# W1 in thirds, the first two tiles in column pieces, and the final waits on GpSimd: one change to a linear-attention and MLP kernel

## Chip, cores, metric

One core of one Trainium2 chip. The metric is the device time of one execution in microseconds (us), and lower is better.

## The reference, cut to what matters

```python
x = A_x                                  # 1 x 2048 x 640, bf16
xn = _layernorm(x, axis=-1)
return x + _A_ref(xn, A_wqkv, A_wo) + _B_ref(xn, B_w1, B_b1, B_w2, B_b2)

def _B_ref(x, w1, b1, w2, b2):           # w1: 640 x 1536, w2: 1536 x 640
    h = _gelu(x @ w1 + b1)               # gelu, tanh form
    return h @ w2 + b2
# _A_ref: q, k, v = xn @ wqkv; linear attention over 32 heads of 20; times wo   [cut]
```

The 2048 tokens are 16 tiles of 128 tokens. The W1 stage (h = gelu(xn W1 + b1)) comes first; the K projection follows, then the rest of the attention, the Q projection, and last the product with W2 together with the output of the attention.

## The kernel before

A small planner records the instructions of each engine in order, and sets semaphores between them. The parts that matter here, with cuts marked `[...]`:

```python
NW1 = 4                                            # W1 by quarters of its columns
dma_x(0, 1)                                        # SyncE's queue
dma_w("scalar", b1tmp[:], ...)                     # ScalarE's queue
dma_w1(0, "scalar"); dma_x(1, 1); dma_w1(1); dma_x(2, 1); dma_w1(2); dma_x(3, 1); dma_w1(3)
[...]
filler(10)                                         # 128x512 matmuls on zeros
ln_stats(0); ln_half(1, 0); ln_half(1, 1); ln_aggr(1)
norm0(0, CA, r_xnA); norm0(CA, D, r_xnB)           # tile 0 normalised, 256 + 384 columns
dA, sA, bA = transp0(0, 2, r_xnA); filler(1); dB, sB, bB = transp0(2, DT, r_xnB)
Pl.ins(v, lambda e: e.tensor_copy(dA, sA), ...)                      # first piece: VectorE
Pl.ins("scalar", lambda e: e.activation(dB, sB, ACT.Copy), ...)      # second piece: ScalarE
b1_step()
ln_norm(1)                                         # tile 1 whole
h_first([0, 1, 2])                                 # tile 0, column blocks 0-2 of W1, k 0-1 then 2-4
[...]
xnT_copy(1, transp(1)); ln_stats(2); ln_next(2)
units(0, 1, 3, 2 * JQ)                             # units(first tile, tiles, blocks lo, hi)
units(1, 1, 0, 2 * JQ)
units(0, 2, 2 * JQ, 2 * JQ + 2)
[...]
stores = [...]
for ev in stores[:-1]:
    Pl.wait_event("scalar", ev)
Pl.wait_event("sync", stores[-1])
```

`h_first` and `units` are matmuls with the weights W1[k, block] and, as moving operand, the transposed normalised tokens of one, two or four tiles: 128, 256 or 512 columns.

## Time and profile before

The first three executions took 207.98, 208.29 and 207.98 us; the profiled one has a span of 206.8 us. The first two lines are the head and the busy times of the page of the kernel before; the third, from its part 4, is the chain of work that ended last, by engine.

```profile
span 206.8 us, 3936 instructions
PE 203.7 (98%) x1588; PEld 140.6 (68%) x1588; DVE 112.2 (54%) x231; ACT 73.2 (35%) x141; POOL 21.2 (10%) x59
...
PE 96%; DMA 3%; ACTq 0%; DVE 0%; issue 0%
```

TensorE (PE) is busy nearly all the time, and the chain is made of it. The chain in order of time (start, duration, what) shows the one thing ahead of TensorE's stream:

```profile
0.80 0.63 ACTq L233
1.43 0.04 issue
1.46 5.52 DMA W<-in_B_w_dram
6.99 0.05 issue
7.03 1.07 PE ps L382 x15
8.10 0.28 PE ps L336 x5
...
60.42 21.73 PE ps L473 x160
```

The first real matmul starts at 7.03 us, released by the first quarter of W1, which landed at 6.99. From there TensorE hardly waits (0.07 us in its first group of matmuls, by start times). How the first tile gets ready meanwhile is in the timeline (start, duration, engine, line, operation; the bracket is idle time before it and what ended it):

```profile
4.42 0.57 POOL L318 TENSOR_TENSOR rstd<-aggr,mhalf 128x1 f32<-128x1 f32 x1 [0.48 <-DVE aggr L316]
5.22 0.21 DVE L316 BATCH_NORM_AGGREGATE aggr<-stats 128x2 f32<-128x12 f32 x1
5.35 0.71 DVE L365 TENSOR_SCALAR xn_tm<-xPK,aggr,rstd 128x256 bf16<-128x256 bf16 x2
5.70 0.39 PE L372 MATMUL ps<-ident,xn_tm 128*128 128x128 bf16 x2
6.87 0.49 ACT L405 ACTIVATE xnT<-ps 128x384 bf16<-128x384 bf16 x1 [3.48 <-PE ps L372]
```

The power that gives 1/sqrt(variance) is ready at 4.99, but normalising starts at 5.35: VectorE (DVE) first does tile 1's aggregate. The second copy, on ScalarE, ends only at 7.36. So even without W1's wait the front has little to spare.

The spacing of matmuls, worked out from their start times in the trace, tells what each form costs in a full stream, and when the clock steps:

```
kernel before, spacing of successive matmuls
fillers, 128x512, up to 6.3 us    427 ns
128 columns, after 7.03 us         55.8 ns
256 columns                       109.2 ns
512 columns                       215.8 ns
```

A 512-column matmul takes 427 ns early and 215.8 later: the clock runs at half rate at first. The trace's clock record puts the step at 6.77 us. The page's PEclk row does not show it: it has 9 tenths in its first slice as in all others.

### The profile page before, as it was taken

The numbers are of one execution on the slowest core, as the hardware profiler recorded it, in microseconds if no ns is written. First come the engines' busy times: TensorE is split into PE (matmuls) and PEld (weight loads), VectorE is DVE, ScalarE is ACT, GpSimd is POOL, SyncE is SP. The second block draws the span as 40 slices with busy tenths as digits, with TensorE's granted clock in tenths as the row PEclk, the third lists the DMA queues.
The fourth block names the chain that finished last, engine by engine and source line by source line (L and its number), as shares of the span: only waits on it lengthen the run. The fifth ranks groups of instructions, "written<-read, shape, count | busy, mean of one in ns | idle before, by whom it ended". The sixth has DMA issues, their size and how long they took to land.

```text
span 206.8 us, 3936 instructions
## 1 busy us (share of the span) xinstructions
PE 203.7 (98%) x1588; PEld 140.6 (68%) x1588; DVE 112.2 (54%) x231; ACT 73.2 (35%) x141; POOL 21.2 (10%) x59
## 2 busy tenths in 40 slices
PE   7999999999999999999999999999999999999996
PEld 2799987444457777777756556677777777777775
DVE  4679970000006888999288888574763522522332
ACT  2589887666676555111153554400000000000000
POOL 3245568000022000000000000000000000000000
PEclk9999999999999999999999999999999999999999
DMA  6999668998000000000300001932112112000002
GB/s 167 344 357 114 105 126 138 375 325 277 3 0 0 0 0 3 0 3 0 63 0 5 0 0 23 370 120 51 63 67 57 55 43 57 32 33 35 32 33 65
DMA packets 23851, 18.32 MB, mean 89 GB/s; under 512 B 10392, under 2 KB 23832, under 8 KB 23832
## 3 DMA queue, kind: packets, MB, share of 16 engines
q1 hardware_dynamic: 23152, 17.57, 30.1%
q10 hardware_dynamic: 680, 0.49, 0.9%
q8 instruction: 12, 0.20, 0.4%
q14 instruction: 7, 0.06, 0.1%
HBM read 12.62 MB, written 2.62 MB: 74 GB/s over the span
## 4 chain that ended last, share of the span: by engine, by line
PE 96%; DMA 3%; ACTq 0%; DVE 0%; issue 0%
PE ps L615 34%; PE ps L352 25%; PE ps L512 11%; PE ps L473 11%; PE ps L524 10%; DMA W<-in_B_w_dram 3%; PE ps L651 2%; PE ps L551 1%; PE ps L533 1%; PE ps L562 1%; PE ps L382 1%; PE ps L336 0%; ACTq L233 0%; DVE out_sb L654 0%
## 5 line engine op out<-in xcount | busy, mean ns | idle before, releaser
L352 PE MATMUL ps<-xnT,W 128*128 128x128 bf16 (+2 forms) x435 | 52.0, 282 | 0.0
L615 PE MATMUL ps<-W,HG 128*128 128x320 bf16 x360 | 51.0, 299 | 0.0
L352 PEld LDWEIGHTS ps<-xnT,W 128*128 128x128 bf16 x435 | 35.6, 98 | 15.6
L615 PEld LDWEIGHTS ps<-W,HG 128*128 128x128 bf16 x360 | 35.1, 98 | 14.2 <-issue 0.4
L356 ACT ACTIVATE HG<-ps,b1c 128x128 bf16<-128x128 f32 (+2 forms) x87 | 40.1, 493 | 12.4 <-PE ps L352 10.3
L634 DVE TENSOR_TENSOR out_sb<-ps,xnT 128x640 bf16<-128x640 f32 x15 | 12.4, 825 | 35.0 <-PE ps L615 34.8
L460 ACT ACTIVATE ek<-ps 128x512 bf16<-128x512 f32 (+1 forms) x36 | 23.2, 645 | 20.3 <-PE ps L524 10.6
L461 DVE TENSOR_SCALAR ek<-ek 128x512 bf16<-128x512 bf16 (+1 forms) x36 | 11.0, 304 | 33.7 <-ACT ek L460 32.5
L615 PE MATMUL ps<-Msb,PQ 128*128 128x320 bf16 x150 | 22.3, 299 | 0.0
L524 PE MATMUL ps<-xnT,Wqkv 128*128 128x512 bf16 x100 | 21.9, 379 | 0.0
L512 PE MATMUL ps<-xPK,xn_tm 128*128 128x320 bf16 x160 | 21.9, 299 | 0.0
L473 PE MATMUL ps<-Wqkv,xnT 128*128 128x320 bf16 x160 | 21.9, 299 | 0.0
L473 PEld LDWEIGHTS ps<-Wqkv,xnT 128*128 128x128 bf16 x160 | 15.7, 98 | 6.2
L512 PEld LDWEIGHTS ps<-xPK,xn_tm 128*128 128x128 bf16 x160 | 15.7, 98 | 6.1
L615 PEld LDWEIGHTS ps<-Msb,PQ 128*128 128x128 bf16 x150 | 14.7, 98 | 5.7
L524 PEld LDWEIGHTS ps<-xnT,Wqkv 128*128 128x128 bf16 x100 | 11.7, 117 | 9.5
L463 DVE SCALAR_TENSOR_TENSOR PQ<-ps,ek 128x512 bf16<-128x512 f32 x20 | 13.8, 692 | 2.1
L308 DVE BATCH_NORM_STATS2 stats<-xPK 128x6 f32<-128x320 bf16 x32 | 13.6, 467 | 1.9 <-DMA xPK<-in_A_x_dram 1.9
L463 DVE SCALAR_TENSOR_TENSOR xPK<-ps,ek 128x640 bf16<-128x640 f32 x16 | 13.2, 824 | 1.7
L499 DVE TENSOR_TENSOR Msb<-Msb,xPK 128x640 f32<-128x640 f32 x14 | 11.6, 826 | 0.5
L318 POOL TENSOR_TENSOR rstd<-aggr,mhalf 128x1 f32<-128x1 f32 x16 | 9.1, 569 | 8.9 <-DVE aggr L316 8.9
L516 ACT ACTIVATE W<-ps 128x640 bf16<-128x640 f32 x5 | 3.5, 704 | 18.2 <-PE ps L512 18.2
(61 smaller groups left out, 94.6 us busy)
## 6 DMA issues: line engine op xcount, KB each, us to landing
xnT<-in_A_x_dram SPq DMA_DIRECT2D x4, 640.0 KB, 6.2
Wqkv<-in_A_wqkv_dram SPq DMA_DIRECT2D x3, 800.0 KB, 6.5
out_dram<-out_sb SPq DMA_DIRECT2D x15, 160.0 KB, 1.8
W<-in_B_w_dram SPq DMA_DIRECT2D x1, 1920.0 KB, 15.2
W<-in_B_w_dram SPq DMA_DIRECT2D x3, 480.0 KB, 6.7
xPK<-in_A_x_dram SPq DMA_DIRECT2D x2, 640.0 KB, 9.0
Wo<-in_A_wo_dram SPq DMA_DIRECT2D x1, 800.0 KB, 10.4
xPK<-in_A_x_dram SPq DMA_DIRECT2D x4, 160.0 KB, 4.1
```

The lines of the kernel that those rows point to most:

```text
L308: Pl.ins(v, lambda e: e.bn_stats(stats[:, s, 6 * h:6 * h + 6], x_in[:, t, h * HW:(h + 1) * HW]), reads=[r_x[t]], writes=[r_stats[s][h]])
L352: Pl.ins("tensor", [(lambda e, k=k: e.matmul(bank(b, 0, w), W1[:, k, jb * P:(jb + 1) * P], xnT[:, k, tok], start=(k == 0), stop=(k == DT - ...
L356: Pl.ins("scalar", lambda e: e.activation(HG[:, jb, tok], bank(b, 0, w), ACT.Gelu_apprx_tanh, bias=b1c[:, jb:jb + 1]), reads=[B_[b], r_b1c ...
L460: Pl.ins("scalar", lambda e: e.activation(e2, src, ACT.Exp), reads=br, writes=[r_ek[s]])
L461: Pl.ins(v, lambda e: e.tensor_scalar(et, et, 1.0, 1e-6, ALU.min, ALU.add), reads=[r_ek[s]], writes=[r_ek[s]])
L463: Pl.ins(v, lambda e: e.scalar_tensor_tensor(out=d2, in0=src, scalar=0.0, in1=e2, op0=ALU.max, op1=ALU.add), reads=br + [r_ek[s]], writes= ...
L473: fns.append(lambda e, k=k, h=h, b=b, t=t: e.matmul(bank(b + h, 0, HW), xnT[:, k, t * P:(t + 1) * P], Wqkv[:, k, D + h * HW:D + (h + 1) * ...
L499: Pl.ins(v, lambda e, t=t: e.tensor_tensor(out=zsum, in0=zsum, in1=PK[:, t, :], op=ALU.add), reads=[r_PK[t], r_zsum], writes=[r_zsum])
L512: Pl.ins("tensor", [(lambda e, t=t, h=h, b=b, f=f: e.matmul(bank(b + h, 0, HW), xn_tm[:, t, f * P:(f + 1) * P], PK[:, t, h * HW:(h + 1) * ...
L524: Pl.ins("tensor", [(lambda e, k=k, j=j, b=b: e.matmul(bank(b), Wqkv[:, k, j:D:DT], xnT[:, k, cc], start=(k == 0), stop=(k == DT - 1))) fo ...
L615: return lambda e: e.matmul(bank(b + h, 0, HW), l, r[:, h * HW:(h + 1) * HW], start=(i == 0), stop=(i == JT + DT - 1))
L634: Pl.ins(v, lambda e: e.tensor_tensor(out=halves(out_sb[:, s, :]), in0=pair(b), in1=halves(x_res[:, t, :]), op=ALU.add), reads=B_[b:b + 2] ...
```

## The change

The intent: let the first real matmul start earlier, keep TensorE supplied while tile 1 is prepared, and use fewer, wider matmuls. The first third of W1 comes in two DMAs (two of five row blocks by ScalarE's queue, three by SyncE's). Tiles 0 and 1 are both normalised, transposed and copied in two column pieces, with tile 1's transposes set between tile 0's matmuls. The copies of tile 0 change engines. b1's transpose moves up among the fillers. Several pairs of 128-column matmuls become one of 256. And GpSimd, instead of ScalarE, waits for the last stores but one.

```diff
-        NW1 = 4
+        NW1 = 3
-        dma_w1(0, "scalar")
+        dma_w("scalar", W1[:, 0:KA, 0:FW], w1v[:, 0:KA, 0:FW], r_W1A)          # KA = 2
         dma_x(1, 1)
+        dma_w("sync", W1[:, KA:DT, 0:FW], w1v[:, KA:DT, 0:FW], r_W1[0])
         dma_w1(1)
[...]
-        filler(10)
+        filler(6)
+        b1_step()
+        filler(3)
         ln_stats(0)
         ln_half(1, 0)
         ln_half(1, 1)
+        norm_part(0, 0, CA, r_xnA)
+        norm_part(0, CA, D, r_xnB)
         ln_aggr(1)
-        norm0(0, CA, r_xnA)
-        norm0(CA, D, r_xnB)
[...]
-        Pl.ins(v, lambda e: e.tensor_copy(dA, sA), ...)
-        Pl.ins("scalar", lambda e: e.activation(dB, sB, ACT.Copy), ...)
-        b1_step()
-        ln_norm(1)
-        h_first([0, 1, 2])
+        Pl.ins("scalar", lambda e: e.activation(dA, sA, ACT.Copy), ...)
+        Pl.ins(v, lambda e: e.tensor_copy(dB, sB), ...)
+        norm_part(1, 0, CA, r_xnA1)
+        norm_part(1, CA, D, r_xnB1)
+        h_first(0, [0, 1, 2, 3], r_xnTA, {1: lambda: copy_part(0, 2, r_xnA1, r_xnTA1),
+                                          3: lambda: copy_part(2, DT, r_xnB1, r_xnT[1])})
+        h_first(1, [0, 1, 2, 3], r_xnTA1)
[...]
-        units(0, 1, 3, 2 * JQ)
-        units(1, 1, 0, 2 * JQ)
-        units(0, 2, 2 * JQ, 2 * JQ + 2)
+        units(0, 2, JQ, 2 * JQ + 1)
[... likewise tiles 2 and 3, and 4 and 5; VectorE's order of statistics and normalising changes with them]
         for ev in stores[:-1]:
-            Pl.wait_event("scalar", ev)
+            Pl.wait_event("gpsimd", ev)
```

More of the change, by code (lines that the diff above doesn't have):

```diff
@@ L204, in bass_parallel_sum__linear_attn_block__dense_activation_gelu__prompt_kernel @@
         r_xnT = [R_("xnT%d" % t) for t in range(NT)]
-        NW1 = 4
+        NW1 = 3
+        r_W1A = R_("W1_0A")
         r_W1 = [R_("W1_%d" % i) for i in range(NW1)]
@@ L239, in dma_w1 @@
             dma_w(eng, W1[:, :, i * FW:(i + 1) * FW], w1v[:, :, i * FW:(i + 1) * FW], r_W1[i])
+        KA = 2
         dma_x(0, 1)
         dma_w("scalar", b1tmp[:], B_b1.rearrange("(a p) -> a p", p=P), r_b1tmp)
-        dma_w1(0, "scalar")
+        dma_w("scalar", W1[:, 0:KA, 0:FW], w1v[:, 0:KA, 0:FW], r_W1A)
         dma_x(1, 1)
+        dma_w("sync", W1[:, KA:DT, 0:FW], w1v[:, KA:DT, 0:FW], r_W1[0])
         dma_w1(1)
@@ L247, in bass_parallel_sum__linear_attn_block__dense_activation_gelu__prompt_kernel @@
         dma_x(3, 1)
-        dma_w1(3)
         dma_x(4, 2)
@@ L362, in bass_parallel_sum__linear_attn_block__dense_activation_gelu__prompt_kernel, with norm_part, transp_part @@
         r_xnA, r_xnB = R_("xn0A"), R_("xn0B")
-        def norm0(lo, hi, res):
-            Pl.ins(v, lambda e: e.tensor_scalar(xn_tm[:, 0, lo:hi], x_in[:, 0, lo:hi], aggr[:, 0, 0:1], rstd[:, 0:1],
+        def norm_part(t, lo, hi, res):
+            s = t % 4
+            Pl.ins(v, lambda e: e.tensor_scalar(xn_tm[:, t, lo:hi], x_in[:, t, lo:hi], aggr[:, s, 0:1], rstd[:, s:s + 1],
                                                 ALU.subtract, ALU.mult),
-                   reads=[r_x[0], r_aggr[0], r_rstd[0]], writes=[res, r_xn[0]])
-        def transp0(k0, k1, res):
+                   reads=[r_x[t], r_aggr[s], r_rstd[s]], writes=[res, r_xn[t]])
+        def transp_part(t, k0, k1, res):
             b = take(1)
@@ L372, in transp0 @@
             Pl.ins("tensor", [(lambda e, k=k: e.transpose(pT[:, (k - k0) * P:(k - k0 + 1) * P],
-                                                          xn_tm[:, 0, k * P:(k + 1) * P], ident[:]))
+                                                          xn_tm[:, t, k * P:(k + 1) * P], ident[:]))
                               for k in range(k0, k1)],
                    reads=[res, r_ident], writes=[B_[b]])
-            return xnT[:, k0:k1, 0:P], pT[:, 0:(k1 - k0) * P].rearrange("p (k q) -> p k q", k=k1 - k0), b
@@ L378, in h_first @@
-        def h_first(jbs):
+            return xnT[:, k0:k1, t * P:(t + 1) * P], pT[:, 0:(k1 - k0) * P].rearrange("p (k q) -> p k q", k=k1 - k0), b
+        def h_first(t, jbs, resA, between=None):
             bs = [take(1) for _ in jbs]
-            for (ks, res) in (((0, 1), r_xnTA), ((2, 3, 4), r_xnT[0])):
-                for jb, b in zip(jbs, bs):
+            tok = slice(t * P, (t + 1) * P)
+            for (ks, res) in (((0, 1), resA), ((2, 3, 4), r_xnT[t])):
+                for i, (jb, b) in enumerate(zip(jbs, bs)):
@@ L382, in h_first @@
                     Pl.ins("tensor", [(lambda e, k=k, jb=jb, b=b: e.matmul(
-                        bank(b, 0, P), W1[:, k, jb * P:(jb + 1) * P], xnT[:, k, 0:P],
+                        bank(b, 0, P), W1[:, k, jb * P:(jb + 1) * P], xnT[:, k, tok],
                         start=(k == 0), stop=(k == DT - 1))) for k in ks],
-                        reads=[r_W1[jb * P // FW], res], writes=[B_[b]])
+                        reads=[r_W1A if res is resA else r_W1[jb * P // FW], res], writes=[B_[b]])
@@ L386, in h_first @@
+                    if between and res is not resA and i in between:
+                        between[i]()
             for jb, b in zip(jbs, bs):
                 Pl.ins("scalar", lambda e, jb=jb, b=b: e.activation(
-                    HG[:, jb, 0:P], bank(b, 0, P), ACT.Gelu_apprx_tanh, bias=b1c[:, jb:jb + 1]),
-                    reads=[B_[b], r_b1c], writes=[r_HG[0][jb]])
-        r_xnTA = R_("xnT0A")
+                    HG[:, jb, tok], bank(b, 0, P), ACT.Gelu_apprx_tanh, bias=b1c[:, jb:jb + 1]),
@@ L392, in bass_parallel_sum__linear_attn_block__dense_activation_gelu__prompt_kernel @@
+                    reads=[B_[b], r_b1c], writes=[r_HG[t][jb]])
+        r_xnTA, r_xnTA1 = R_("xnT0A"), R_("xnT1A")
+        r_xnA1, r_xnB1 = R_("xn1A"), R_("xn1B")
         Pl.ins("scalar", lambda e: e.activation(b1c[:, 0:1], warm[:, 0:1], ACT.Gelu_apprx_tanh),
                reads=[r_warm], writes=[r_b1c])
-        filler(10)
+        filler(6)
+        b1_step()
+        filler(3)
         ln_stats(0)
@@ L397, in bass_parallel_sum__linear_attn_block__dense_activation_gelu__prompt_kernel, with copy_part @@
         ln_half(1, 1)
+        norm_part(0, 0, CA, r_xnA)
+        norm_part(0, CA, D, r_xnB)
         ln_aggr(1)
-        norm0(0, CA, r_xnA)
-        norm0(CA, D, r_xnB)
-        dA, sA, bA = transp0(0, 2, r_xnA)
+        dA, sA, bA = transp_part(0, 0, 2, r_xnA)
         filler(1)
-        dB, sB, bB = transp0(2, DT, r_xnB)
-        Pl.ins(v, lambda e: e.tensor_copy(dA, sA), reads=[B_[bA]], writes=[r_xnTA])
-        Pl.ins("scalar", lambda e: e.activation(dB, sB, ACT.Copy), reads=[B_[bB]], writes=[r_xnT[0]])
-        b1_step()
-        ln_norm(1)
-        h_first([0, 1, 2])
+        dB, sB, bB = transp_part(0, 2, DT, r_xnB)
+        Pl.ins("scalar", lambda e: e.activation(dA, sA, ACT.Copy), reads=[B_[bA]], writes=[r_xnTA])
+        Pl.ins(v, lambda e: e.tensor_copy(dB, sB), reads=[B_[bB]], writes=[r_xnT[0]])
+        norm_part(1, 0, CA, r_xnA1)
+        norm_part(1, CA, D, r_xnB1)
+        def copy_part(k0, k1, res, dst):
+            d, s, b = transp_part(1, k0, k1, res)
+            Pl.ins(v, lambda e: e.tensor_copy(d, s), reads=[B_[b]], writes=[dst])
+        h_first(0, [0, 1, 2, 3], r_xnTA, {1: lambda: copy_part(0, 2, r_xnA1, r_xnTA1),
+                                          3: lambda: copy_part(2, DT, r_xnB1, r_xnT[1])})
+        h_first(1, [0, 1, 2, 3], r_xnTA1)
         TD = 4
@@ L421, in ln_next @@
                 ln_half(t + 1, 0)
-                ln_half(t + 1, 1)
             ln_norm(t)
             if t + 1 < NT:
+                ln_half(t + 1, 1)
                 ln_aggr(t + 1)
-        xnT_copy(1, transp(1))
+        units(0, 2, JQ, 2 * JQ + 1)
         ln_stats(2)
-        ln_next(2)
-        units(0, 1, 3, 2 * JQ)
-        units(1, 1, 0, 2 * JQ)
-        units(0, 2, 2 * JQ, 2 * JQ + 2)
+        ln_norm(2)
+        ln_stats(3)
         xnT_copy(2, transp(2))
-        units(0, 2, 2 * JQ + 2, JT)
+        units(0, 2, 2 * JQ + 1, JT)
         ln_next(3)
+        units(2, 1, 0, 3)
+        xnT_copy(3, transp(3))
+        units(2, 1, 3, 6)
         ln_next(4)
-        units(2, 1, 0, JQ)
-        xnT_copy(3, transp(3))
-        units(2, 1, JQ, JT)
-        units(3, 1, 0, JT)
+        units(3, 1, 0, 6)
+        units(2, 2, 6, JT)
         for t in range(TD, NT):
@@ L447, in bass_parallel_sum__linear_attn_block__dense_activation_gelu__prompt_kernel @@
         run_masks(len(mask_jobs))
-        for (t0, n) in [(4, 2), (6, 2), (8, 4), (12, 4)]:
+        units(4, 1, 0, 3)
+        units(5, 1, 0, 3)
+        units(4, 2, 3, JT)
+        for (t0, n) in [(6, 2), (8, 4), (12, 4)]:
             units(t0, n, 0, JT)
```

## The prediction

> **What bounds the kernel now.** The page's first part shows TensorE busy for 203.7 of 206.8 us, and the chain of waits is 96% TensorE: one unbroken stream from the first real matmul (7.03 us) to the last. Ahead of it stands one wait, "DMA W<-in_B_w_dram", from 1.46 to 6.98 us: the first quarter of W1, 480 KB on ScalarE's queue. The table of waits shows no later one, so only an earlier start or a shorter stream can pay.
>
> **The stream.** By start times in the trace a matmul takes 55.8 ns with 128 moving columns, 109.2 with 256, 215.8 with 512. The change replaces fifty 128-column matmuls by twenty-five of 256: 50 x 55.8 - 25 x 109.2 = 0.06 us saved. [...] Transposes: 15 before in the stream, 15 after. So the regrouping is worth almost nothing to TensorE.
>
> **The start.** The first DMA becomes 262 KB. In the trace ScalarE's queue had moved 184 packets by 4.0 us and 351 by 4.5, so its 256 packets should land near 5.0 us. The first matmul then waits for normalisation and transposition of tile 0. DVE's first normalising piece no longer waits behind the second aggregate: 5.35 -> about 5.1. Transposes follow 0.34 later (5.69 -> 5.43), and the first copy moves to ScalarE, starting about 5.87. Its duration, estimated from the copies of 384 columns (492 ns) and 12 (170 ns): 0.38. First real matmul about 6.3 instead of 7.03: 0.73 us earlier.
>
> **What is given back.**
> - The clock. The fillers (128x512) come every 427 ns, half rate, and the spacing becomes 56 ns only at about 6.77 us. [...] Matmuls between 6.3 and 6.8 should run at 107 ns: 0.24 us lost.
> - Tile 1's copies between the pieces: waits of about 0.04 and 0.14 us; one of 0.07 in the old first group goes. Net 0.1.
> - The rest of the first third (393 KB, SyncE's queue) should land at 6.0 to 6.8; it is needed near 7.0. If late, 0 to 0.3 us.
>
> W1's later thirds should land near 8.5 and 10.9 us, needed near 9.5 and 11.7. Tiles 4 and 5's DMA transposes move later by 1.3 to 1.7 us, to about 19.8 and 21.1, needed at about 21.0 and 21.9: no wait, thin margin.
>
> **The end.** Moving the waits from ScalarE to GpSimd touches neither the last store nor SyncE's wait for it (206.82). 0 us, unless GpSimd ends more slowly.
>
> **Sum.** 0.73 + 0.06 - 0.24 - 0.1 = 0.45 us saved: 207.5 us, range 206.8 to 208.2. Chances: faster by over 2% 0.005, within 2% 0.985, slower by over 2% 0.01.
>
> **What would show it.** In the timeline: first real matmul at 6.2 to 6.4, released by ScalarE's copy and not by a DMA; its first matmuls 107 ns apart up to about 6.8; the K matmuls beginning about 59.8 instead of 60.26; W1's second piece landed by 6.9. In the table of waits: TensorE's waits in the first 25 us below 0.4 us in sum.
>
> **What would make it wrong.** W1's second piece or a later third landing late; tile 5's transpose late (wait near 22 us); the clock's step falling elsewhere, which moves either kernel by some 0.3 us; GpSimd prolonging the program's end.

The 107 ns are in the trace of the kernel before: its transposes, of 128 columns, start 107 ns apart between 6.31 and 6.52 us. The 0.24 us, and the "some 0.3 us" for a step elsewhere, are estimates from that spacing and the step at 6.77 us.

## The result, and the profile after

Ratios here are computed as the mean time of one kernel's fast executions over that of the other's from the same rounds, so they are not quite the ratio of the medians quoted beside them. Executions over 1.5% slower than the fastest of the same kernel are left out of the means. The changed kernel was run in three sets:

| set | changed, median us (range, n) | before, median us (n) | ratio (95%) |
|---|---|---|---|
| first | 207.98 (207.59 to 208.43, 6) | 208.05 (6) | 0.9994 (0.9981 to 1.0008) |
| second (`after_again`) | 207.94 (207.70 to 208.06, 5) | 208.31 (11) | 0.9978 (0.9965 to 0.9991) |
| third (`after_third`) | 207.99 (207.77 to 208.55, 6) | 208.31 (11) | 0.9975 (0.9936 to 1.0014) |

So the time is the same within 2%, by a wide margin. A gain of 0.1 to 0.4 us in the medians is likely; the second set alone separates it from nothing.

The page and the chain of the changed kernel (the profiled execution of the first set), to be set against those of before:

```profile
span 206.3 us, 3886 instructions
PE 202.4 (98%) x1562; PEld 139.7 (68%) x1562; DVE 114.1 (55%) x233; ACT 72.5 (35%) x136; POOL 21.4 (10%) x59
...
PE 96%; DVE 1%; DMA 1%; issue 0%; DVEq 0%
```

```profile
0.80 2.33 DMA xPK<-in_A_x_dram
...
5.12 0.36 DVE xn_tm L368
5.48 0.05 issue
5.53 0.28 PE ps L375 x2
...
6.38 0.94 PE ps L386 x14
...
59.84 21.73 PE ps L491 x160
```

The wait for W1 is gone from the chain; in its place stands the landing of tile 0 of x, and then tile 0's own preparation. ScalarE has 136 instructions, five fewer. In the timeline:

```profile
4.45 0.57 POOL L320 TENSOR_TENSOR rstd<-aggr,mhalf 128x1 f32<-128x1 f32 x1 [0.48 <-DVE aggr L318]
5.12 0.76 DVE L368 TENSOR_SCALAR xn_tm<-xPK,aggr,rstd 128x256 bf16<-128x256 bf16 x2
5.53 0.28 PE L375 MATMUL ps<-ident,xn_tm 128*128 128x128 bf16 x2 [0.66 <-DVE xn_tm L368]
5.80 0.20 DVE L318 BATCH_NORM_AGGREGATE aggr<-stats 128x2 f32<-128x12 f32 x1
5.85 0.38 ACT L413 ACTIVATE xnT<-ps 128x256 bf16<-128x256 bf16 x1 [1.52 <-PE ps L375]
6.38 0.94 PE L386 MATMUL ps<-xnT,W 128*128 128x128 bf16 x14
```

Normalising now starts as soon as the power is there, ScalarE's copy takes the 0.38 us that was estimated, and the first real matmul follows at 6.38. The next two answers cut both kernels at the first real matmul and at the first matmul of the K projection (stretch, its length, then busy us and instruction count of each engine). Before:

```profile
7.03:60.26 53.23, 53.23 (x466) 37.29 (x466) 19.98 (x59) 40.66 (x91) 16.00 (x46) 1.00 0.75 198
60.26:206.80 146.54, 144.75 (x1107) 101.27 (x1105) 88.62 (x161) 30.90 (x48) 2.77 (x1) 1.00 0.14 43
```

After:

```profile
6.38:59.68 53.30, 53.30 (x441) 36.97 (x441) 22.44 (x63) 39.54 (x84) 16.56 (x47) 1.00 0.69 200
59.68:206.30 146.62, 144.75 (x1107) 101.32 (x1105) 88.65 (x161) 30.89 (x48) 2.77 (x1) 1.00 0.14 43
```

The W1 stage has 25 matmuls fewer and takes as long as before: 53.30 against 53.23 us. The rest is unchanged. All of the gain, 0.58 us to the K projection in this pair of traces, is the earlier first matmul. The trace's start times also show that in this execution the clock had stepped to full rate by 4.05 us (fillers 216 ns apart after it), so no early matmul ran slowly. That raised the first question: was the good trace merely a lucky one?

### The profile page after: what moved, and what is told of

Same layout as the page of the kernel before. It is cut to its first block, busy times and chain, and to the rows that moved or that the text cites. A ratio compares the mean times of both kernels' runs of the same rounds, so it can differ in the third digit from the quotient of the medians.

```text
span 206.3 us, 3886 instructions
## 1 busy us (share of the span) xinstructions
PE 202.4 (98%) x1562; PEld 139.7 (68%) x1562; DVE 114.1 (55%) x233; ACT 72.5 (35%) x136; POOL 21.4 (10%) x59
## 4 chain that ended last, share of the span: by engine, by line
PE 96%; DVE 1%; DMA 1%; issue 0%; DVEq 0%
PE ps L633 34%; PE ps L354 24%; PE ps L530 11%; PE ps L491 11%; PE ps L542 10%; PE ps L669 2%; PE ps L569 1%; PE ps L386 1%; DMA xPK<-in_A_x_dram 1%; DVE stats L310 1%; PE ps L551 1%; PE ps L580 1%; PE ps L375 0%; PE ps L338 0%; DVE xn_tm L368 0%
## 5 line engine op out<-in xcount | busy, mean ns | idle before, releaser
L354 PE MATMUL ps<-xnT,W 128*128 128x256 bf16 (+2 forms) x385 | 50.5, 293 | 0.0
L354 PEld LDWEIGHTS ps<-xnT,W 128*128 128x128 bf16 x385 | 33.9, 98 | 15.9
L358 ACT ACTIVATE HG<-ps,b1c 128x256 bf16<-128x256 f32 (+2 forms) x77 | 38.0, 516 | 12.7 <-PE ps L354 10.3
L479 DVE TENSOR_SCALAR ek<-ek 128x512 bf16<-128x512 bf16 (+1 forms) x36 | 10.9, 304 | 25.9 <-ACT ek L478 24.8
L310 DVE BATCH_NORM_STATS2 stats<-xPK 128x6 f32<-128x320 bf16 x32 | 14.7, 470 | 2.5 <-DMA xPK<-in_A_x_dram 2.5
```

Source lines behind the costliest of these rows:

```text
L310: Pl.ins(v, lambda e: e.bn_stats(stats[:, s, 6 * h:6 * h + 6], x_in[:, t, h * HW:(h + 1) * HW]), reads=[r_x[t]], writes=[r_stats[s][h]])
L354: Pl.ins("tensor", [(lambda e, k=k: e.matmul(bank(b, 0, w), W1[:, k, jb * P:(jb + 1) * P], xnT[:, k, tok], start=(k == 0), stop=(k == DT - ...
L358: Pl.ins("scalar", lambda e: e.activation(HG[:, jb, tok], bank(b, 0, w), ACT.Gelu_apprx_tanh, bias=b1c[:, jb:jb + 1]), reads=[B_[b], r_b1c ...
L479: Pl.ins(v, lambda e: e.tensor_scalar(et, et, 1.0, 1e-6, ALU.min, ALU.add), reads=[r_ek[s]], writes=[r_ek[s]])
```

## Experiments

The first four ran on one chip, and shared their executions of the kernel before (median 208.31, range 207.83 to 208.72).

### after_again: the changed kernel unaltered

> The changed kernel unaltered, for another trace and a spread of spans. In its one profile the K projection began 0.58 us earlier than before (59.68 against 60.26), the span was 0.5 us shorter, and yet the six times differ by 0.06% in the mean. Theory A (the clock): that profile fell on an execution in which TensorE's clock stepped to full rate at about 3.9 us; where it steps later, the first matmuls run at half rate and the gain shrinks. A expects spans between 206.3 and 206.9 us, and, if this trace shows a late step (after 6.4 us), first matmuls 107 ns apart and a start of the K projection at 59.8 to 60.0. Theory B (the end): the start's gain is there in every execution and GpSimd's waits lengthen what comes after the last instruction: B expects spans of 206.2 to 206.4 in all executions and time minus span larger than before by 0.3 to 0.5. Theory C (the loads): a piece of W1 or a DMA transpose lands late in some executions: C expects a wait of TensorE of 0.2 us or more inside the first 30 us of this trace.

Measured: 207.94 us, spans 206.4 to 206.8; the kernel before had spans from 206.6 to 207.5 beside it. The clock stepped at 6.04 us, the first real matmul came at 6.48, at 56 ns spacing, and the K projection at 59.80. Time minus span was 1.26 to 1.40 us, against 1.22 to 1.31 for before.

So no early matmul ran at half rate here either, although the clock stepped 2 us later than in the first trace: theory A in its strong form is not needed. Theory B fails, for what follows the last instruction is longer by less than 0.1 us. There was no wait inside the W1 stage, so C has no support either. The gain is simply there, and small against the spread of the kernel before.

### end_scalar and end_gpsimd: the last part of the change, undone and alone

```diff
 # end_scalar: on the changed kernel            # end_gpsimd: on the kernel before
-            Pl.wait_event("gpsimd", ev)         -            Pl.wait_event("scalar", ev)
+            Pl.wait_event("scalar", ev)         +            Pl.wait_event("gpsimd", ev)
```

> The changed kernel with the waits for all but the last store moved back to ScalarE. Theory A: same time as the changed kernel within 0.1 us (0.05%). Theory B: faster than the changed kernel by 0.3 to 0.5 us, thus a ratio to the kernel before of about 0.9975. Theory C says nothing of it: same.

> The kernel before with only the last part of the change: GpSimd waits for all but the last store. Theory A and C: the same as before within 0.1 us (ratio 0.9995 to 1.0005). Theory B: slower by 0.3 to 0.5 us, ratio 1.0015 to 1.0025, with the span unchanged at about 206.8.

Measured: end_scalar 208.48 us (208.17 to 208.80), ratio to before 1.0006 (0.9992 to 1.0021); end_gpsimd 208.32 us, ratio 1.0002 (0.9986 to 1.0017).

No theory had foreseen end_scalar: with ScalarE waiting, the changed kernel is *slower* by 0.5 us than with GpSimd (medians 208.48 and 207.94, ranges that do not overlap), while in the kernel before the same move does nothing. The front of end_scalar's trace is as good as the changed kernel's (first matmul 6.46, K projection 59.73), and VectorE's last operation starts at 204.52 against 204.59 in after_again; but the span is 206.9 against 206.4. The half microsecond is lost after the last computation. The DMA view of end_scalar between 205.7 and 206.3 us, while the last store's packets pass (queue and kind: packets, MB, share of 16 engines):

```profile
DMA packets 134, 0.04 MB, mean 64 GB/s; under 512 B 133, under 2 KB 133, under 8 KB 133
...
q1 hardware_dynamic: 133, 0.03, 23.6%
q14 instruction: 1, 0.01, 4.0%
```

One packet of 8,192 bytes of *instructions* (trace: start 205.76 us, 380 ns) runs among the packets of the store. In the traces each store has 16 reports of landing, and the program ends after the last of them; of this store fifteen come by 206.29 and the last at 206.91, at the end of the span of 206.9. In after_again there is no such packet in that time, and the sixteenth comes 0.02 us after the fifteenth.

This gave theory F, to be tested below: ScalarE's instructions arrive in blocks, of which the packet of 8,192 bytes would be one, as its program advances. The regrouping takes five instructions out of ScalarE's program (141 to 136), so each later instruction sits five places earlier in its blocks, and a block that had been fetched long before the end is now fetched at the very end, if ScalarE still has its final waits to execute. The kernel before has an instruction packet at 185.85 us that end_gpsimd lacks. It comes 1.3 us after ScalarE's wait at 184.56; in end_scalar the packet comes 1.0 us after ScalarE's wait at 204.76, which is five wait instructions further down the list.

### no_fill: the changed kernel without its first nine fillers

```diff
-        filler(6)
         b1_step()
-        filler(3)
```

> The changed kernel without its first nine filler matmuls, so TensorE does nothing before about 5.4 us. Theory A: the first real matmul keeps its place (about 6.35 us) but matmuls run 107 ns apart until the clock steps, at some 9 to 12 us; half the rate for 2.5 to 5.5 us costs 1.2 to 2.8 us: time about 209 to 210.5. If the clock's early state did not matter (B, C): no change, ratio 1.000.

Measured: 209.34 us, ratio 1.0050 (1.0033 to 1.0066). In the trace the first real matmul came at 6.67 us, matmuls ran 107 ns apart until 10.5 us, and the K projection began at 61.62, 1.8 us later than in after_again. The clock's early state costs what was expected when the fillers are missing. The expected step at 9 to 12 us was the author's estimate; the two traces at hand had it at 4.05 us or earlier (changed) and at 6.77 (before), 2.8 us or less and 5.5 us after the first filler at 1.25. In the changed kernel they are there, and its three traces show the step at 4.05 or earlier, at 6.04 and at 5.67 us: always ahead of the first real matmul.

### end_scalar_pad and before_fetch: theory F, both ways

These, with the next two, ran on another chip (before: median 208.25, range 207.94 to 210.08). The first keeps ScalarE's waits and puts five tiny instructions back into its program. The second takes five wait instructions out of ScalarE's program in the kernel *before*, by giving ten of its waits to GpSimd.

```diff
 # end_scalar_pad: end_scalar, and ahead of the K projection's first activation
+        for i in range(5):
+            Pl.ins("scalar", lambda e, i=i: e.activation(scr[:, i:i + 1], warm[:, i:i + 1], ACT.Copy), reads=[r_warm])
 # before_fetch: on the kernel before
-        for ev in stores[:-1]:
-            Pl.wait_event("scalar", ev)
+        for i, ev in enumerate(stores[:-1]):
+            Pl.wait_event("gpsimd" if i < 10 else "scalar", ev)
```

> Waits back on ScalarE as in end_scalar, plus five tiny ScalarE copies in the idle stretch before the K projection (scratch output). Theory F (fetch): [...] in end_scalar such a block was loaded at 205.76 us, in the midst of the last store's packets, and one of the store's 16 landings came 0.6 us after the others. In the kernel before the same block came at 185.9 us, because ScalarE had five instructions more ahead of it. F expects: the block at about 185, none after 205, the last store's 16 landings within 0.2 us of each other, and the time back at that of the changed kernel: ratio to before 0.997 to 0.999. Rival S: ScalarE's waiting itself is slow to end the program; then the time stays as in end_scalar, ratio about 1.0006, span 206.9 to 207.5.

> The kernel before, with ten of the 21 waits moved from ScalarE to GpSimd, which takes five instructions out of ScalarE's stream ahead of the last wait. Theory F: the block at 185.9 us moves to about 206.3, into the last store: slower than before by 0.2 to 0.6 us, ratio 1.001 to 1.003, one landing of the last store late. Rival S: fewer waits on ScalarE, so the same or faster than before.

That the block is ScalarE's was theory F; what shows it is below.

Measured: end_scalar_pad 207.83 us (207.56 to 207.97), ratio to before 0.9972 (0.9943 to 1.0002): five instructions more make the kernel faster than end_scalar. before_fetch 209.08 us (208.85 to 209.80), ratio 1.0036 (1.0007 to 1.0065): fewer waits on ScalarE make the kernel slower, more than F's 0.2 to 0.6 us, and every one of its six executions is slower than ten of the eleven of before. The block of end_scalar_pad, in its DMA view from 184 to 186 us:

```profile
DMA packets 1, 0.01 MB, mean 4 GB/s; under 512 B 0, under 2 KB 0, under 8 KB 0
...
q14 instruction: 1, 0.01, 1.7%
```

And that of before_fetch, from 206.4 to 207.2 us, among the last store's packets:

```profile
DMA packets 142, 0.04 MB, mean 50 GB/s; under 512 B 141, under 2 KB 141, under 8 KB 141
...
q1 hardware_dynamic: 141, 0.03, 18.9%
q14 instruction: 1, 0.01, 4.0%
```

```
kernel           last ScalarE block at   last store: 15th and 16th report
before           185.85                  206.78  206.80
end_scalar       205.76                  206.29  206.91
end_scalar_pad   185.07                  206.25  206.28
before_fetch     206.53                  207.00  207.77
changed          none in this stretch    206.20  206.23
```

Rival S expected the first to stay as slow as end_scalar and the second to lose nothing, and falls. The packets do not name the engine whose instructions they carry; that the block is ScalarE's is shown by these four kernels, in which only ScalarE's and GpSimd's programs were edited (against their parents) and it moved as ScalarE's program did: the traces hold 197 records of ScalarE, its waits included, where the block comes at 185 (before, end_scalar_pad), and 192 where it falls in the last store (end_scalar, before_fetch). In end_scalar and before_fetch one report of the 16 is late, by 0.6 and 0.8 us, with one packet of 8,192 bytes among the store's. The traces kept here do not name the engine of a packet, and the packets themselves took only 0.38 and 0.51 us, so how the delay arises is not shown. A part of before_fetch's loss (its K projection began at 60.46) is its front, not its end.

All 14 traces agree with a collision. Of the last four stores of each, 56 in all, eleven have an instruction packet of 8,192 bytes starting 0.57 to 0.97 us after the store's issue, and in these the sixteenth report comes 0.21 to 0.77 us after the fifteenth; in the other 45 it comes within 0.07 us. The changed kernel has one too, at 204.50 us (after_again 204.60), but it falls in the last store but one, whose late report holds up nothing. That packet stays near 204.5 us whether ScalarE has 181, 192 or 197 records (changed, end_scalar, end_scalar_pad), and seems to go with SyncE's program: with 84, 83, 82 and 81 SyncE records (before_split, before, changed, one_dma) it comes at about 198.3, 202.69, 204.50 and 206.40 us. So ScalarE is probably not the only engine whose blocks can collide with a store. This was read from the traces afterwards; no run was made to test it.

### before_split and one_dma: what W1's first load is worth

```diff
 # before_split: on the kernel before
-        dma_w1(0, "scalar")
+        dma_w("scalar", W1[:, 0:KA, 0:FW], w1v[:, 0:KA, 0:FW], r_W1A)
         dma_x(1, 1)
+        dma_w("sync", W1[:, KA:DT, 0:FW], w1v[:, KA:DT, 0:FW], r_W1[0])
 # one_dma: on the changed kernel, the first third whole
-        dma_w("scalar", W1[:, 0:KA, 0:FW], ...)
+        dma_w1(0, "scalar")
         dma_x(1, 1)
-        dma_w("sync", W1[:, KA:DT, 0:FW], ...)
```

> The kernel before, with only the first quarter of W1 fetched by two DMAs (two of five row blocks on ScalarE's queue, three on SyncE's). In the two traces of the old start the quarter landed at 6.99 and 6.30 us and the first real matmul came at 7.03 and 6.56. If the load is what sets the old start in some executions and the normalising chain in the others: first real matmul at 6.5 to 6.65 us, released by the chain, K projection from 59.75 to 59.95, ratio to before 0.997 to 0.999. If the load does not matter: no change, ratio 1.000.

> The changed kernel, with its first third of W1 (655 KB) in one DMA on ScalarE's queue. If splitting is what makes the early start possible: the third lands at 7.2 to 7.9 us, the first real matmul waits for it, the K projection begins at 60.6 to 61.2, ratio to before 1.001 to 1.004. If the first load is off the chain: first matmul at 6.4, ratio as the changed kernel, 0.998.

Measured: before_split 208.10 us, ratio 1.0003 (0.9962 to 1.0043). Its two loads landed at 4.95 and 5.34 us, yet the first real matmul came at 6.92, stopped again for ScalarE's second copy, and the K projection began at 60.37: later than expected, and no gain in the trace. Here the clock stepped at 7.04, so fillers and transposes ran at half rate to the end (ten fillers took 4.45 us, as in the kernel before), and the order of the old front did the rest. In this trace, then, the split alone did not bring the start forward; what it gives when the clock steps earlier was not seen. The times do not settle it: the medians differ by 0.15 us, and the interval does not exclude the expected gain.

one_dma: 210.55 us (executions from 208.84 to 210.64, one at 212.24), ratio 1.0073 (1.0032 to 1.0114). The trace is of the 208.84 us execution; the third landed at 7.17 us, and TensorE's table of waits has

```profile
PE ps L295 <- DVE warm L263: 1.3, 1, 1.3
```

in the kernel before, and in one_dma

```profile
PE ps L296 <- DVE warm L264: 1.3, 1, 1.3
PE ps L385 <- DMA W<-in_B_w_dram: 0.6, 1, 0.6
```

The first real matmul came at 7.21 and the K projection at 60.51, about 0.7 us after that of the changed kernel and a little ahead of the expected range. So the split is needed for the early start of the changed kernel. But the load is not all of the loss: with one DMA fewer in SyncE's program the packet described above comes at 206.40 us, in the last store, whose sixteenth report is 0.40 us late (207.16 and 207.56). That is a third of the 1.2 us by which this span is longer than that of after_again. And the ratio lies above the expected 1.001 to 1.004 because three other executions took 1.6 to 1.8 us longer than the traced one; no trace shows why.

### tile1_whole and regroup: the pieces and the wider matmuls

These ran on the chip of the first four (before: median 208.31, range 207.89 to 210.94).

```diff
 # tile1_whole: on the changed kernel
-        norm_part(1, 0, CA, r_xnA1)
-        norm_part(1, CA, D, r_xnB1)
+        ln_norm(1)
-        h_first(0, [0, 1, 2, 3], r_xnTA, {1: ..., 3: ...})
+        h_first(0, [0, 1, 2, 3], r_xnTA, {3: copy_whole})      # five transposes, one copy
 # regroup: on the kernel before, waits on GpSimd
-        units(0, 1, 3, 2 * JQ)
-        units(1, 1, 0, 2 * JQ)
-        units(0, 2, 2 * JQ, 2 * JQ + 2)
+        units(1, 1, 0, 3)
+        units(0, 2, 3, 8)
 [... and tiles 2 and 3 likewise]
```

> The changed kernel with tile 1 normalised, transposed and copied whole, its five transposes standing together after the first group. If the pieces matter: TensorE waits some 0.5 us for the copy before it begins tile 1's matmuls, so the K projection begins about 0.5 us later than in the changed kernel (60.2 instead of 59.7 to 59.8), ratio to before 1.000 to 1.001. If they do not: 59.7 to 59.8, ratio 0.998.

> The kernel before with waits on GpSimd (so that ScalarE's block of instructions cannot hit the last store) and only a regrouping of the W1 matmuls: ninety of 128 columns become forty-five of 256, more than in the change. By the spacings 90 x 55.8 - 45 x 109.2 = 0.11 us: from the first real matmul to the first of the K projection 53.1 us instead of 53.2 to 53.4, ratio to before 0.999 to 1.000. If fewer weight loads mattered to TensorE (98 ns of weight load each, 45 fewer), 1 us or more would go: 52.2 us or less, ratio 0.995.

Measured: tile1_whole 208.51 us, ratio 1.0010 (0.9963 to 1.0056); K projection at 60.63 in the trace. TensorE's waits, then the chain around the copy:

```profile
PE ps L386 <- DVE xnT L420: 0.6, 1, 0.6
```

```profile
8.05 0.29 PE ps L338 x5
8.34 0.02 issue
8.37 0.50 DVE xnT L420
8.87 0.05 issue
8.92 1.29 PE ps L386 x20
```

By start times TensorE stood for 0.75 us (five transposes and the gap after them took 1.03 us, where five transposes take 0.28). That is somewhat more than the half microsecond expected. The K projection was later still because here the clock stepped at 6.90, after the first matmul at 6.50: the first twenty matmuls took 1.39 us, and 1.11 in after_third, where they ran at full rate throughout. Of the 0.28 us, 0.18 went to the half-rate spacing before 6.90 and 0.09 to a wait at 7.07. Among the traces of the new front with its fillers and loads in place, this is the one in which the predicted loss to the clock is seen.

regroup: 208.90 us, ratio 1.0018 (0.998 to 1.0056); from the first real matmul to the K projection 53.82 us instead of the expected 53.1. TensorE's waits:

```profile
PE ps L382 <- DMA W<-in_B_w_dram: 0.8, 1, 0.8
PE ps L352 <- DVE xnT L344: 0.6, 1, 0.6
```

The expectation was a miss, and its cause is the same copy: in the kernel before, fifteen 128-column matmuls of tile 0 stand between tile 1's transposes and its first use, and merging them into wider ones takes that cover away. TensorE stood for 0.75 us. Taken off, 53.07 us are left, against 53.16 of before (53.23 less the 0.07 that its first group waited): 0.09 us saved, as 90 x 55.8 - 45 x 109.2 = 0.11 says. Fewer weight loads bring no more.

### x0_halves: an attempt to beat both

```diff
-        dma_x(0, 1)
-        dma_w("scalar", b1tmp[:], ...)
+        # tile 0 of x: columns 0-319 by SyncE's queue, 320-639 by ScalarE's; b1 by GpSimd, after the identity
```

> A version meant to beat both: the changed kernel with tile 0 of x fetched as two column halves, one on SyncE's and one on ScalarE's queue, and b1 fetched by GpSimd. In the changed kernel the start is set by x's tile landing at 3.12 to 3.19 us, then statistics, GpSimd's power, normalisation, transposes and copy up to 6.38 to 6.48. If the tile's landing bounds the start: halves land at 2.7 to 2.9 us, first real matmul at 6.0 to 6.2, gain over the changed kernel 0.1 to 0.3 us (less where the clock still runs at half rate), ratio to before 0.996 to 0.998. If two queues share one rate, so the halves land no earlier, or GpSimd's fetch delays its power: no gain, ratio as the changed kernel.

Measured: 210.88 us, ratio 1.0114 (1.0070 to 1.0158). A failure, twice over. The halves landed at 3.18 and 3.36 us, no earlier than the whole tile (3.12 to 3.14 in the changed kernel's three traces). And b1, fetched by GpSimd, landed at 6.49 us, 4.6 us after its issue (by ScalarE's queue at 2.6, 1.8 us after), while its transpose had kept its place among the fillers:

```profile
PE ps L305 <- DMA b1tmp<-in_B_b_dram: 2.5, 1, 2.5
```

TensorE stood for it in order, and everything shifted: first real matmul 8.90, and the first fourteen, up to 10.36, at half rate (107 ns apart). The wait was an oversight in the edit; the landings show that the idea would not have paid without it.

### after_third: the changed kernel once more

> The changed kernel unaltered on this chip, beside the three above. Expected as in the first two sets: ratio to before 0.9975 to 0.9995, spans 206.3 to 206.9, first real matmul at 6.35 to 6.5 us wherever the clock steps before it, last store's landings close together.

Measured: 207.99 us, ratio 0.9975 (0.9936 to 1.0014), spans 206.4 to 207.2, one of the six above the expected 206.9. First real matmul 6.43, clock step 5.67, K projection 59.81, the last two reports of the last store 0.02 us apart.

## Why the prediction was right or wrong

It was right in the main: 207.5 us, with a range of 206.8 to 208.2, and 207.98 came out. The mechanism was the predicted one, a stream of TensorE that nothing shortens behind a front that can be moved a little. The number says little by itself: the range also holds the 208.05 us of the kernel before, so no gain at all would have fallen inside it. And there was luck in it: the move of the waits, put at 0 us, turned out to save what the regrouping would have lost at the end. Without it, by end_scalar's ratio, the time would have been about 208.2 us, an estimate, at the upper edge of the range. Point by point:

- **The start.** "First real matmul about 6.3 instead of 7.03: 0.73 us earlier." It came at 6.38, 6.48 and 6.43, 0.55 to 0.65 us earlier than 7.03. But the 7.03 was one draw: the old front, unaltered up to that matmul, shows 6.56, 7.03, 7.28 and 7.46 in four traces (end_gpsimd, before, before_fetch, regroup), after landings of W1's first quarter from 6.30 to 7.41. The new front is steadier as well as earlier.
- **The clock.** "Matmuls between 6.3 and 6.8 should run at 107 ns: 0.24 us lost." This term was mis-sized. It took the step's time, 6.77, from a single trace. The changed kernel's three traces have it by 4.05, at 6.04 and at 5.67, and lost nothing. The mechanism exists: 0.18 us went that way in tile1_whole.
- **Tile 1's pieces.** Predicted waits of 0.04 and 0.14 us; the first trace has gaps of 0.05 and 0.11. tile1_whole shows what they prevent, 0.75 us.
- **The stream.** "The regrouping is worth almost nothing to TensorE": 53.30 against 53.23 us, and 0.09 us measured in regroup once its wait is taken off. But merging also takes away the matmuls that covered tile 1's copy, so the pieces are what makes the merging affordable. That link was not in the prediction.
- **The loads.** W1's first piece, predicted near 5.0 us, landed at 5.68, 4.58 and 5.86 in the three traces, ahead of its first use in each. Its second piece landed at 6.19, 6.07 and 6.63 (predicted 6.0 to 6.8), the later thirds at 8.3 and 10.7 in the first trace (8.5 and 10.9). The DMA transposes of tiles 4 and 5 landed at 18.99 and 20.81 and were needed at 20.64 and 21.48: no wait. "TensorE's waits in the first 25 us below 0.4 us" was wrong as written: the view lists 0.7 us ahead of the first transposes, because the fillers ended early once the clock had stepped. It cost nothing.
- **The end.** "0 us, unless GpSimd ends more slowly." True of the move by itself (end_gpsimd 1.0002), and wrong of the move within the change. The step that failed is "touches neither the last store": the regrouping, without the move, puts ScalarE's block of instructions into the last store (0.62 us late in end_scalar), and the change comes out at 1.0006 instead of 0.9978. The last part does not add a gain; it removes a loss that the rest of the change would have brought.

On the size: the terms as measured in the first pair of traces (0.65 us at the start, 0.07 given back in the stream, 0.58 in the span by unrounded times) exceed the predicted 0.45. Over all traces the K projection begins at 60.22 on average with the unaltered old front (before, end_gpsimd, before_fetch) and at 59.75 with the new one (the three of the changed kernel, end_scalar, end_scalar_pad): 0.47 us. The medians of the times show 0.07, 0.37 and 0.32. What fills the difference is open: only the profiled execution of each kernel has a trace, and the others spread by up to 0.9 us, with a rare one 2 us longer. The landing of W1 (its first quarter at 6.30 to 7.41 us with the old front), the clock's step (4.05 us or earlier to 7.04 with the fillers in place) and the last reports of stores (up to 0.77 us after the fifteenth) all vary from trace to trace by tenths and more, which could account for the spread, but that is argued and not shown.

## What to carry to other kernels

Where one engine's stream fills the span, ask of a change only whether it shortens that stream or starts it earlier, and do not size the start from one trace: look at several, since a load's landing and the clock's step move by tenths and more (here 6.30 to 7.41 us, and 4.05 or earlier to 7.04). When an edit adds or removes instructions of an engine that is still active at the very end, look at the instruction packets around the last store; a few instructions more or less, or other hands for the last waits, can be worth half a microsecond (208.48 us in end_scalar; 207.83 in end_scalar_pad, 207.94 in after_again). Before merging small matmuls, check which copy they were covering (TensorE stood 0.75 us for it in regroup).
